# Where the buffers lie in SBUF: LayerNorm's little tiles go to the front, and 192 bytes are left free behind the x buffers

## The chip, the core and the metric

The kernel runs on one NeuronCore of a Trainium2 chip. The metric is device time in microseconds of one launch, from its begin to its end on the chip. The median of the runs is 721.3 us.

## What is computed

x is [2048, 512]. The rows are normalized, then go two ways: a Fourier mixing (a product with the 512-point DFT along the hidden axis and with the 2048-point DFT along the sequence, of which the real part is kept) and an MLP of width 1792 with a squared ReLU. The second gates the first.

```python
xn = _layernorm(x)                                # over the 512 features
a, b = xn @ dft_hid_re.T, xn @ dft_hid_im.T
s = dft_seq_re @ a - dft_seq_im @ b               # [2048, 512]
h = max(xn @ w1 + b1, 0) ** 2                     # [2048, 1792]
g = silu(h @ w2 + b2)
out = x + s * g
```

All inputs are float32.

## The kernel before

Nearly everything is a matmul of 128 x 128 weights (the stationary operand, read by a LDWEIGHTS of its own for each MATMUL) with 256 or 512 moving columns, both in float32 words ("fp32r") and both read from SBUF. To keep float32's precision, every operand is held as two parts, HI and LO, and every product is three passes: HI by HI, HI by LO, LO by HI. ScalarE writes HI (line 68) and VectorE LO (line 71). Most products also follow a scheme for 2 x 2 blocks that needs seven products instead of eight: the blocks and their sums are stored side by side in a buffer of seven slots. TensorE's order is written out by hand; the engines wait for each other by semaphores.

The stages, in order of time:

- **LayerNorm and the first two column chunks** (line 330, 384 matmuls of 512 columns). Stationary: the normalized x in eight buffers `XC[0..7]` (tags `xc0`..`xc7`, 14336 bytes in each partition). Moving: pieces of the sequence DFT matrix in the buffers `g1a`, `g1b`.
- **The other six column chunks** (function `mm`, line 277, 2016 matmuls of 256 columns; six chunks of eight steps of 42). Stationary: `XC`. Moving: products 1, 2, 3 take theirs from `g0a`/`g0b`, products 4, 5, 6, 7 from `g1a`/`g1b`. VectorE and ScalarE prepare the moving operands two steps ahead.
- **The hidden DFT** (`stage2`, line 263, 384 matmuls of 512 columns, laid between the steps of the others). Stationary: results of the stages above in the buffers `pq00`..`pq11`. Moving: the DFT matrix in `wd0`, `wd1`.
- **The first MLP layer** (`hidden`, line 517, 1176 matmuls of 256 columns): 4 token chunks of 7 units of 42. Stationary: w1, of which units 0 to 5 lie in `xc2`..`xc7` and unit 6 in `g0b` (3 slots, `w1a`) and `g1b` (4 slots, `w1b`). Moving: the normalized tokens `xT`, in `xc0`, `xc1` for chunks 0 and 2 and in `wd0`, `wd1` for chunks 1 and 3.
- **The second MLP layer** (`outer`, line 571, 1176 matmuls of 256 columns): 4 chunks of 7 units of 42. Stationary: h in `xc4`, `xc5`, `xc6`. Moving: w2, of which units 0 to 4 lie in `xc0`, `xc1`, `xc7`, `xc2`, `xc3` and units 5 and 6 in `wd0`, `wd1`.

One pool holds all of SBUF. It gives each tag its place the first time the tag is used, one behind the other, rounded up to 32 bytes. So the order in which tags first appear in the program settles every address. In the program before, `ln_stats` asks for its tile `bn` (three copies of 48 bytes, each on 64) and `ln_root` for `sm` (three copies of 16 bytes, each on 32) after `g0b` and before `g1a` have been placed: these 288 bytes lie between the two.

Of the kernel before, what the change touches and what calls it, by code (L numbers as in the profile page):

```python
# [7 lines left out]
F32 = mybir.dt.float32  # L8
# [4 lines left out]
P = 128  # L13
# [48 lines left out]
def fnet_gated_kernel(ctx, tc, x, xt, ct, wd, w1, w2, b1, b2, out):  # L62
# [10 lines left out]
    def split(*parts):  # L73
        split_hi(*parts)
        return split_lo(*parts)

    pool = ctx.enter_context(tc.tile_pool(name="pool", bufs=1))
# [17 lines left out]
    def buf(tag, shape, name, dtype=F32, bufs=1):  # L95
        return pool.tile(shape, dtype, tag=tag, bufs=bufs, name=name)

    def bcast(src, n):
        return bass.AP(tensor=src.tensor, offset=src.offset, ap=[[0, P], [1, n]])

    def halves(ap):
        return ap.rearrange("p (a b) -> p a b", a=2)


    XC = [buf(f"xc{j}", [P, 7, 2, 256], f"xc{j}", F32R) for j in range(NJ)]

    xr, xn32 = {}, {}

# [5 lines left out]

    def ln_stats(j, hs=slice(0, 2)):
        t = xr[j]
        sm = buf("bn", [P, 12], f"bn{j}_{hs.start}", bufs=3)
        for h in range(hs.start, hs.stop):
            bn = sm[:, 6 * h:6 * h + 6]
            nc.vector.bn_stats(bn, t[:, h])  # L120
            nc.vector.bn_aggr(stats[:, :, h, j], bn)

    root = {}

    def ln_root(j, hs=slice(0, 2)):
        n = hs.stop - hs.start
        t = root[j] = buf("sm", [P, 4], f"root{j}_{hs.start}", bufs=3)
        nc.scalar.activation(t[:, 0:n], stats[:, 1, hs, j], AF.Sqrt, bias=eps)

    def ln_rstd(j, hs=slice(0, 2)):  # L130
# [17 lines left out]
    def xc_parts(j, h):  # L148
        s = slice(2 * h, 2 * h + 2)
        return XC[j][:, s, HI, :], XC[j][:, s, LO, :], halves(xn32[j][:, h])  # L150

# [12 lines left out]
    def split_sums(j):  # L164
        s = xn32[j].rearrange("p h (b n) -> p (h b) n", b=2)
        split(XC[j][:, S2:S4 + 1, HI, :], XC[j][:, S2:S4 + 1, LO, :], s[:, 0:3])

    def split_s1(j):
        split(XC[j][:, S1, HI, :], XC[j][:, S1, LO, :], s1[j // ND][:, j % ND])

# [46 lines left out]
    def product(ms, n):  # L217
        m26, m753, m4, m1 = ms
        return {1: m1, 4: m4, 2: m26[:, 0], 6: m26[:, 1], 7: m753[:, 0], 5: m753[:, 1], 3: m753[:, 2]}[n]
# [30 lines left out]
    def pq(c, m, dh, src=None):  # L250
        t = PQ[c, m, dh] = buf(f"pq{m}{dh}", [P, 2, 512], f"pq{c}_{m}_{dh}", F32R)
        if src is not None:
            split(t[:, HI], t[:, LO], src)
        return t
# [18 lines left out]
    def mm(ps, w, mv, first, last):  # L273

        for d in range(2):
            for a_, b_ in PASSES:
                nc.tensor.matmul(ps[:, d * CW:(d + 1) * CW], w[:, a_, d * P:(d + 1) * P], mv(b_),  # L277
                                 start=first and d == 0 and (a_, b_) == (HI, HI),
                                 stop=last and (a_, b_) == (LO, HI), skip_group_check=True)
# [3 lines left out]
    def load_rows(c, t):  # L283

        flat = rows.rearrange("a b -> (a b)")
        for m in range(2):
            for h in range(2):
                n = m * S + c * TC + h * 256
                nc.sync.dma_start(t[:, 2 * m + 1 - h], bcast(flat[n:n + 256], 256))
        xT["rows"] = t  # L290
# [32 lines left out]
    def products(c, j, h, by_pass=False):  # L323

        g = part[c, j]
        for passes in [[q] for q in PASSES] if by_pass else [PASSES]:
            for k in range(ND):
                for a_, b_ in passes:
                    w = XC[j][:, 2 * h + k // 2, a_, k % 2 * P:(k % 2 + 1) * P]
                    nc.tensor.matmul(accs[c][k], w, g[:, b_, 2 * h:2 * h + 2],  # L330
# [6 lines left out]
    with tc.manual_schedule(engines=None):  # L337
# [10 lines left out]
        for n, (count, dtype) in enumerate(zip(WARM, (mybir.dt.bfloat16, F32R))):  # L348
            zeros = buf("g0" + "ab"[n], [P, 512], f"zeros{n}", dtype)
            nc.vector.memset(zeros if n == 0 else zeros.bitcast(F32), 0.0)  # L350
            for _ in range(count):
                nc.tensor.matmul(warm, zeros[:, 0:P], zeros, start=True, stop=True)
        plain_banks(0)
        ln_stats(0, one)
        ln_root(0, one)
        for h, hs in enumerate((one, two)):
            g = plain_parts(0, 0, hs)
            split_hi(*g)
            ln_rstd(0, hs)
            ln_xn(0, h)  # L360
            split_hi(*xc_parts(0, h))
            if h == 0:
                ln_stats(0, two)
                ln_root(0, two)
            split_lo(*g)
            if h == 1:
                ln_stats(1)
                g = plain_parts(0, 1)
                split_hi(*g)
                ln_root(1)  # L370
            split_lo(*xc_parts(0, h))
            products(0, 0, h, True)
        load_c(0, 3)
        load_x(4)
        for j in range(1, NJ):
            ln_rstd(j)
            for h in range(2):
                ln_xn(j, h)
                split_hi(*xc_parts(j, h))
            split_lo(*g)  # L380
            load_c(*order[j + 3])
            if j + 4 < NJ:
                load_x(j + 4)
            split_lo(*xc_parts(j, 0))
            if j + 1 < NJ:
                ln_stats(j + 1)
                ln_root(j + 1)
            xn_lo = split_lo(*xc_parts(j, 1))
            for h in range(2):
                products(0, j, h, j == 1)  # L390
            g = plain_parts(*order[j + 1])
            split_hi(*g)
            if j == 2:
                nc.sync.dma_start(b1s, b1)
                nc.sync.dma_start(b2s, bcast(b2, D))
        split_lo(*g)

    for n, (c, j) in enumerate(order):
# [20 lines left out]
        if j == NJ - 1:  # L419
            for dh in range(2):  # L420
                for m in range(2):
                    t = pq(c, m, dh)
# [216 lines left out]
    for c, j in steps:  # L639
# [3 lines left out]
        for p in ORDER:  # L643
            a, (grp, b) = PRODUCTS[p]
            mm(product(ms, p), XC[j][:, a], lambda b_: g[grp][:, b_, b], j == 0, j == NJ - 1)
        if c == PLAIN:
# [14 lines left out]
        if c == NC - 1:  # L661

            if j in (2, 3):
                q = j - 2
                t = buf(f"xc{2 + q}", [P, 3, 4, 256], f"stage{q}")
# [197 lines left out]
def _launch(arrays, out_shape):  # L863
    import numpy as np
    import concourse.bacc as bacc
    from concourse.bass_utils import run_bass_kernel_spmd

    nc = bacc.Bacc("TRN2", target_bir_lowering=False, num_devices=1, dynamic_dma_scratch_size=1024)
    feed, args = {}, []
    for name, v in arrays.items():  # L870
        v = np.ascontiguousarray(v)
        feed[f"in_{name}"] = v
        args.append(nc.dram_tensor(f"in_{name}", v.shape, mybir.dt.from_np(v.dtype), kind="ExternalInput").ap())
    args.append(nc.dram_tensor("out_0", out_shape, F32, kind="ExternalOutput").ap())
    with tile.TileContext(nc, schedule_with_timeline_sim=True) as tc:
        fnet_gated_kernel(tc, *args)
    r = run_bass_kernel_spmd(nc, [feed], core_ids=[0])
    return r.results[0]["out_0"]
# [25 lines left out]
```

## Time and profile before

| | |
|---|---|
| median of 3 runs | 721.3 us (721.28 to 721.83) |
| span of the profiled execution, first to last instruction | 719.5 us |
| TensorE busy with matmuls (PE) | 706.7 us, 5149 matmuls |
| TensorE busy with weight loads (PEld, beside PE) | 665.4 us, 5149 loads |
| VectorE (DVE) | 584.7 us |
| ScalarE (ACT) | 347.6 us |
| HBM read and written | 97.0 MB and 43.3 MB |

The profile is of one execution; its span is 1.8 us under the median of the runs, which also hold what lies before the first and after the last instruction. A matmul's duration in the records includes the time until its last column has left the array, and overlaps the next matmul's; what a matmul costs in a stream is the distance from its start to the next one's start. That is read here from rows of the timeline: the start of a row, the start of the next, and the count between.

### The profile page before, as it was taken

How to read it: one execution, taken by the hardware profiler on the slowest of the kernel's cores; microseconds unless marked ns; L12 is line 12 of the kernel's file. 1: busy time of each engine (PE TensorE's matmuls, PEld its weight loads, DVE VectorE, ACT ScalarE, POOL GpSimd, SP SyncE). 2: the span in 40 equal slices, each digit the busy share in tenths (PEclk: the TensorE clock that was granted, in tenths of full speed). 3: DMA queues.
4: the chain of work that ended last, by engine and by line, in shares of the span. 5: the costliest groups of instructions: out<-in, count | busy, mean ns of one | idle time of the engine just before them, and what ended most of it. 6: DMA issues, size and time to landing. Idle time of an engine off the chain costs nothing.

```text
span 719.5 us, 12692 instructions
## 1 busy us (share of the span) xinstructions
PE 706.7 (98%) x5149; PEld 665.4 (92%) x5149; DVE 584.7 (81%) x886; ACT 347.6 (48%) x475; POOL 5.2 (1%) x8
## 2 busy tenths in 40 slices
PE   8999999999999999999999999999999999999996
PEld 5778789999999999999998999999999999999996
DVE  7999554679598697797795955999988979989895
ACT  4438233434353544444542424777767764444441
POOL 0000000000000000000000000000000000101000
PEclk9999999999999999999999999999999999999999
DMA  9622540633553653744824669965625995767643
GB/s 325 217 88 89 169 137 16 220 107 128 206 205 132 218 189 122 273 152 139 298 92 147 224 243 337 352 248 205 255 112 188 343 405 196 187 205 199 219 146 111
DMA packets 55018, 141.09 MB, mean 196 GB/s; under 512 B 5040, under 2 KB 21680, under 8 KB 53680
## 3 DMA queue, kind: packets, MB, share of 16 engines
q1 hardware_dynamic: 49840, 124.56, 49.5%
q10 hardware_dynamic: 4032, 14.68, 5.2%
q0 software_dynamic: 1088, 1.05, 1.0%
q8 instruction: 40, 0.66, 0.3%
q14 instruction: 18, 0.15, 0.1%
HBM read 97.00 MB, written 43.27 MB: 195 GB/s over the span
## 4 chain that ended last, share of the span: by engine, by line
PE 83%; DVE 12%; issue 2%; ACT 1%; DMA 1%; DVEq 0%; ACTq 0%; SPq 0%
PE m_b L277 24%; PE yps L263 12%; PE m_b_o L571 10%; PE hps L517 9%; PE hps_b L517 5%; PE m_bb L277 5%; PE m_ba L277 5%; DVE g L71 3%; PE pq_b L330 3%; PE hps_ba L517 3%; DVE xc L71 2%; PE m_bc_o L571 1%; PE m_ba_o L571 1%; PE m_bb_o L571 1%; PE hps_bb L517 1%
## 5 line engine op out<-in xcount | busy, mean ns | idle before, releaser
L277 PE MATMUL m_b<-g,xc 128*128 128x256 f32 x1440 | 181.6, 281 | 0.0
L277 PEld LDWEIGHTS m_b<-g,xc 128*128 128x128 f32 x1440 | 175.7, 189 | 0.5
L71 DVE TENSOR_TENSOR g<-r,g 128x768 fp32r<-128x768 f32 (+2 forms) x65 | 65.5, 1007 | 45.4 <-ACT g L68 45.4
L68 ACT ACTIVATE g<-r 128x768 fp32r<-128x768 f32 (+2 forms) x65 | 57.4, 886 | 88.4 <-PE m_b L277 46.3
L263 PE MATMUL yps<-wd,pq 128*128 128x512 f32 x384 | 94.6, 395 | 0.0
L263 PEld LDWEIGHTS yps<-wd,pq 128*128 128x128 f32 x384 | 70.2, 188 | 15.2
L571 PE MATMUL m_b_o<-w,g 128*128 128x256 f32 x630 | 79.3, 282 | 0.5 <-ACT m_b_o L564 0.5
L571 PEld LDWEIGHTS m_b_o<-w,g 128*128 128x128 f32 x630 | 76.9, 191 | 0.7 <-ACT m_b_o L564 0.7
L71 DVE TENSOR_TENSOR g<-t,g 128x1024 fp32r<-128x1024 f32 x48 | 58.7, 1222 | 12.0 <-ACT g L68 12.0
L330 PE MATMUL pq_b<-g,xc 128*128 128x512 f32 x240 | 64.6, 399 | 2.9 <-DVE g L71 1.7
L517 PE MATMUL hps<-xT,w 128*128 128x256 f32 x504 | 61.9, 281 | 0.0
L517 PEld LDWEIGHTS hps<-xT,w 128*128 128x128 f32 x504 | 60.9, 190 | 0.1
L330 PEld LDWEIGHTS pq_b<-g,xc 128*128 128x128 f32 x240 | 44.1, 188 | 17.0 <-ACT xc L68 2.6
L68 ACT ACTIVATE g<-t 128x1024 fp32r<-128x1024 f32 x48 | 50.3, 1048 | 16.7 <-PE m_ba L277 6.8
L528 ACT ACTIVATE h<-h,b1s 128x512 f32<-128x512 f32 x56 | 37.4, 715 | 18.2 <-DVE h L229 18.2
L68 ACT ACTIVATE g<-hr 128x768 fp32r<-128x768 f32 (+1 forms) x28 | 35.5, 1266 | 21.0 <-DVE hr L196 6.7
L71 DVE TENSOR_TENSOR g<-hr,g 128x768 fp32r<-128x768 f32 (+1 forms) x28 | 41.6, 1485 | 2.2 <-ACT g L68 2.1
L277 PE MATMUL m_bb<-g,xc 128*128 128x256 f32 x288 | 43.3, 282 | 0.0
L277 PE MATMUL m_ba<-g,xc 128*128 128x256 f32 x288 | 42.9, 281 | 0.0
L277 PEld LDWEIGHTS m_bb<-g,xc 128*128 128x128 f32 x288 | 39.3, 189 | 1.8
L277 PEld LDWEIGHTS m_ba<-g,xc 128*128 128x128 f32 x288 | 38.1, 189 | 0.1
L188 DVE TENSOR_TENSOR t<-r 128x512 f32<-128x512 f32 x48 | 32.9, 685 | 5.0 <-DMA r<-in_ct 4.8
(167 smaller groups left out, 1007.7 us busy)
## 6 DMA issues: line engine op xcount, KB each, us to landing
r<-in_ct SPq DMA_DIRECT2D x63, 512.0 KB, 3.5
hd<-h ACTq DMA_DIRECT2D x28, 512.0 KB, 4.6
hr<-hd SPq DMA_DIRECT2D x28, 512.0 KB, 4.7
w1d<-w0g SPq DMA_DIRECT2D x21, 512.0 KB, 3.4
w<-w1d SPq DMA_DIRECT2D x6, 1792.0 KB, 9.3
w<-w2d SPq DMA_DIRECT2D x4, 1792.0 KB, 11.4
y<-ysb SPq DMA_DIRECT2D x16, 256.0 KB, 3.1
fin<-y SPq DMA_DIRECT2D x16, 256.0 KB, 5.1
```

Source lines behind the costliest of these rows:

```text
L68: nc.scalar.activation(hi, src, AF.Copy)
L71: return nc.vector.tensor_tensor(lo, src, hi.bitcast(F32), op=ALU.subtract)
L188: nc.vector.tensor_tensor(t[:, 0:2], r[:, 0:1].to_broadcast([P, 2, 256]), r[:, 1:3], op=ALU.add)
L263: nc.tensor.matmul(ps, PQ[c, m, k // 2][:, a_, w:w + P], WD[m, k][:, b_, :], start=n == 0, stop=n == 2 * ND * 3 - 1)
L277: nc.tensor.matmul(ps[:, d * CW:(d + 1) * CW], w[:, a_, d * P:(d + 1) * P], mv(b_), start=first and d == 0 and (a_, b_) == (HI, HI), stop= ...
L330: nc.tensor.matmul(accs[c][k], w, g[:, b_, 2 * h:2 * h + 2], start=j == 0 and h == 0 and (a_, b_) == (HI, HI), stop=j == NJ - 1 and h == 1 ...
L517: nc.tensor.matmul(product(ms, k), W1[p][a][:, a_, q * P:(q + 1) * P], xT[c, q][:, b_, b], start=share not in first, stop=q == 1 and (a_, ...
L528: nc.scalar.activation(x_[:, s], x_[:, s], AF.Relu, bias=b1s[:, f:f + 1])
L571: nc.tensor.matmul(m[:, k * 256:(k + 1) * 256], g[:, a_, a, k * P:(k + 1) * P], W2[p][:, b_, b], start=p == 0 and k == 0 and (a_, b_) == ( ...
```

## The change

The little tiles get their places right behind the statistics, ahead of `XC`, and a tile that nothing reads or writes stands behind `XC`.

```diff
+    small = {tag: [buf(tag, [P, n], f"{tag}_{i}", bufs=3) for i in range(3)] for tag, n in (("bn", 12), ("sm", 4))}
+
+    def few(tag, n, name):
+
+        return small[tag].pop(0) if small[tag] else buf(tag, [P, n], name, bufs=3)
...
     XC = [buf(f"xc{j}", [P, 7, 2, 256], f"xc{j}", F32R) for j in range(NJ)]
+
+    pool.tile([P, 48], F32, name="gap")
...
-        sm = buf("bn", [P, 12], f"bn{j}_{hs.start}", bufs=3)
+        sm = few("bn", 12, f"bn{j}_{hs.start}")
...
-        t = root[j] = buf("sm", [P, 4], f"root{j}_{hs.start}", bufs=3)
+        t = root[j] = few("sm", 4, f"root{j}_{hs.start}")
```

In the built programs, all engines have the same instructions in the same order with the same semaphores and the same addresses in HBM; only SBUF addresses differ. The first byte of a buffer in its partition:

| buffers | before | mod 256 | after | mod 256 |
|---|---|---|---|---|
| `xc0` (`xc1`.. follow at 14336) | 3552 | 224 | 3840 | 0 |
| `pq00`, `r`, `pq01`, `pq10`, `pq11` | 118240.. | 224 | 118720.. | 192 |
| `g0a`, `g0b` | 146912, 153056 | 224 | 147392, 153536 | 192 |
| `bn`, `sm` | 159200.. | | 3552.. | |
| `g1a`, `wd0`, `g1b`, `wd1`, `t`, `e`, `sx` | 159488.. | 0 | 159680.. | 192 |

Every slot that a matmul reads starts at a multiple of 512 bytes within its buffer. So for each stage there is one distance from the stationary to the moving operand, mod 256, whatever the slot:

| stage | stationary, moving | matmuls | columns | before | after |
|---|---|---|---|---|---|
| line 330 | `xc`, `g1` | 384 | 512 | 32 | 192 |
| line 277, products 1, 2, 3 | `xc`, `g0` | 864 | 256 | 0 | 192 |
| line 277, products 4, 5, 6, 7 | `xc`, `g1` | 1152 | 256 | 32 | 192 |
| line 263 | `pq`, `wd` | 384 | 512 | 32 | 0 |
| line 517, chunks 0, 2, units 0 to 5 | `xc`, `xc` | 504 | 256 | 0 | 0 |
| line 517, chunks 1, 3, units 0 to 5 | `xc`, `wd` | 504 | 256 | 32 | 192 |
| line 517, chunks 0, 2, unit 6: `w1a`; `w1b` | `g0b`; `g1b`, `xc` | 36; 48 | 256 | 0; 224 | 64; 64 |
| line 517, chunks 1, 3, unit 6: `w1a`; `w1b` | `g0b`; `g1b`, `wd` | 36; 48 | 256 | 32; 0 | 0; 0 |
| line 571, units 0 to 4 | `xc`, `xc` | 840 | 256 | 0 | 0 |
| line 571, units 5, 6 | `xc`, `wd` | 336 | 256 | 32 | 192 |

## The prediction

> **What bounds the kernel now.** I read the busy times first, then the stretches, then who waited for whom, and last the timeline of TensorE.
>
> ```profile
> PE 706.7 (98%) x5149; PEld 665.4 (92%) x5149; DVE 584.7 (81%) x886; ACT 347.6 (48%) x475; POOL 5.2 (1%) x8
> PEclk9999999999999999999999999999999999999999
> ```
>
> TensorE is busy for 98% of the span at its full granted clock. The stretches (columns: busy time of PE, PEld, DVE, ACT, POOL with counts, then granted clock, DMA share, GB/s) say where the missing 2% is:
>
> ```profile
> 0.00:72.10 72.10, 69.30 (x280) 51.92 (x280) 67.15 (x141) 37.02 (x64) 0.20 (x4) 1.00 0.50 179
> ...
> 112.40:418.70 306.30, 306.30 (x2306) 293.13 (x2305) 237.65 (x352) 132.80 (x179) 0.00 (x0) 1.00 0.49 173
> 418.70:569.60 150.90, 150.90 (x1225) 148.70 (x1225) 126.14 (x184) 96.99 (x135) 0.00 (x0) 1.00 0.67 249
> 569.60:719.50 149.90, 141.22 (x1178) 140.55 (x1176) 130.97 (x175) 68.61 (x80) 4.99 (x4) 0.99 0.65 213
> ```
>
> Up to 72 us VectorE sets the pace (67.15 of 72.10 us). From 112.4 to 569.6 us TensorE never stops, and VectorE has slack: 68.65 of 306.30 us in line 277's stretch, 24.76 of 150.90 us in line 517's. Of the waits that TensorE's matmuls have after the start, these are the longest:
>
> ```profile
> PE pq_b L330 <- DVE g L71: 1.7, 2, 1.3
> PE m L571 <- DVE g L71: 1.3, 1, 1.3
> ```
>
> So no load and no engine is waited for in the long middle. What can change there without any instruction changing is how long a matmul occupies TensorE. The timeline (start, us, row, count) shows that this isn't one number for 256 columns. First the second MLP layer, from the first row of a unit of 42 to the first row of the next:
>
> ```profile
> 580.53 0.88 PE L571 MATMUL m_bb_o<-w,g 128*128 128x256 f32 x6
> ...
> 585.57 0.88 PE L571 MATMUL m_bb_o<-w,g 128*128 128x256 f32 x6
> ...
> 595.65 0.88 PE L571 MATMUL m_bb_o<-w,g 128*128 128x256 f32 x6
> ...
> 600.61 0.87 PE L571 MATMUL m_bb_o<-w,g 128*128 128x256 f32 x6
> ...
> 605.55 0.88 PE L571 MATMUL m_bc_o<-w,g 128*128 128x256 f32 x6
> ```
>
> Unit 2 takes 585.57 - 580.53 = 5.04 us, 120.0 ns a matmul; units 5 and 6 together 605.55 - 595.65 = 9.90 us for 84, 117.9 ns. By the table of distances, unit 2 is at 0 and units 5 and 6 at 32. The first MLP layer says the same of chunk 0 (distance 0) and chunk 1 (distance 32):
>
> ```profile
> 450.00 0.88 PE L517 MATMUL hps_bb<-xT,w 128*128 128x256 f32 x6
> ...
> 455.04 5.20 PE L517 MATMUL hps<-xT,w 128*128 128x256 f32 x42
> ...
> 479.90 0.87 PE L517 MATMUL hps_bb<-xT,w 128*128 128x256 f32 x6
> ...
> 484.85 5.11 PE L517 MATMUL hps<-xT,w 128*128 128x256 f32 x42
> ```
>
> 5.04 us against 4.95 us, again 120.0 and 117.9 ns. That could still be a matter of where the moving operand alone lies. Unit 6 of chunk 1 decides it, since there the stationary operand lies in two places under one and the same moving operand:
>
> ```profile
> 494.75 1.58 PE L517 MATMUL hps<-xT,w1a 128*128 128x256 f32 x12
> 496.16 3.05 PE L517 MATMUL hps<-xT,w1b 128*128 128x256 f32 x24
> 499.04 0.86 PE L517 MATMUL hps<-xT,w1a 128*128 128x256 f32 x6
> ```
>
> `w1a`, at distance 32, takes 1.41 us for 12, 117.5 ns; `w1b`, whose both operands begin at a multiple of 256, takes 2.88 us for 24, 120.0 ns. So alignment as such buys nothing; distance 0 costs 2.1 ns more than distance 32. The loads fit that: 192 ns at distance 0 (`w1a` in chunks 0 and 2), 188 at 32 (`w1a` in chunks 1 and 3) and at 224 (`w1b` in chunks 0 and 2).
>
> ```profile
> L517 PEld LDWEIGHTS hps_ba<-xT,w1a x12: 192/192/193, 460.7 to 531.2; 128*128 128x128 f32 x12
> L517 PEld LDWEIGHTS hps<-xT,w1a x36: 187/188/189, 494.6 to 569.4; 128*128 128x128 f32 x36
> ...
> L517 PEld LDWEIGHTS hps_ba<-xT,w1b x12: 187/188/193, 461.4 to 531.9; 128*128 128x128 f32 x12
> ```
>
> My reading is that the read of the next weights and the stream of the moving columns get in each other's way when they start at the same place of some repeating pattern of SBUF. The Trainium skill has a sentence against this reading, in "TensorE: Matmul & The Clock Gate", section "Step-by-step: what each phase is for": TensorE has two separate read ports, and "Loading the next tile's weights doesn't steal SBUF read bandwidth from the running matmul." By that rule both distances should give one pitch, and the sum below would be 0; the trace disagrees, with 120.0 against 117.9 ns.
>
> **The change part by part.** It adds and removes no instruction, wait or transfer, so the sum is counts by differences in pitch. Line 277 now has a mixture of the two distances, and a step of 42 shows its mean; line 263 has 512 columns:
>
> ```profile
> 245.59 0.88 PE L277 MATMUL m_bb<-g,xc 128*128 128x256 f32 x6
> ...
> 250.57 0.88 PE L277 MATMUL m_bb<-g,xc 128*128 128x256 f32 x6
> ...
> 101.17 5.76 PE L263 MATMUL yps<-wd,pq 128*128 128x512 f32 x24
> 106.77 2.26 PE L330 MATMUL pq_b<-g,xc 128*128 128x512 f32 x9
> ```
>
> 4.98 us a step is 118.6 ns a matmul. For 512 columns it is 5.60 / 24 = 233.3 ns, which is 2 x 116.7: the loads are the same, but have twice the time, so I take 116.7 ns as what 256 columns cost when no weight load holds them up. At distance 32 the pitch of 117.9 still stands 1.2 ns above it.
>
> The unknown is p, the pitch of 256 columns at distance 192, which occurs nowhere in this trace. Its ends are 116.7 ns (no hold-up) and 120.0 ns (the same hold-up as at 0). Four terms follow:
>
> - Line 277, 2016 matmuls: 2016 x (118.6 - p).
> - Line 517, chunks 1 and 3, 504, and line 571, units 5 and 6, 336: 840 x (117.9 - p).
> - Unit 6 of the first MLP layer: 36 `w1a` matmuls of chunks 0 and 2 leave distance 0 and 36 of chunks 1 and 3 come to it, and 48 go from 224 to 64; I put this at nothing, and at 84 x 2.1 = 0.2 us at most.
> - Line 263, 384 matmuls, goes from 32 to 0. Costs lie between 0, if the longer stream covers the later load, and 384 x 2.1 = 0.8 us. I take half, 0.4 us. A gain isn't in it, since no row at distance 0 is faster than one at 32.
>
> Line 330's 384 matmuls go from 32 to 192 under VectorE's pace or at 233.3 ns, the floor as I read it: 0. The other 1344 matmuls of lines 517 and 571 stay at 0.
>
> VectorE and ScalarE read and write at other places too. Two forms of line 71 with equal size and different distances between their operands exist (`t`, `g1`: 0; `r`, `g1`: 32):
>
> ```profile
> L71 DVE TENSOR_TENSOR g<-t,g 128x1024 fp32r<-128x1024 f32 x48 | 58.7, 1222 | 12.0 <-ACT g L68 12.0
> L71 DVE TENSOR_TENSOR g<-r,g 128x1024 fp32r<-128x1024 f32 x15 | 18.3, 1219 | 0.3 <-ACT g L68 0.3
> ```
>
> 3 ns of 1219 on the 15 in VectorE's own stretch are 0.05 us: nothing. For transfers, 512 KB into `e`, a multiple of 256, land no sooner than 512 KB into `r`, 32 under one, so I expect nothing from the new places either:
>
> ```profile
> r<-in_ct SPq DMA_DIRECT2D x63, 512.0 KB, 3.5
> w0raw<-in_w SPq DMA_DIRECT2D x7, 512.0 KB, 4.5
> ```
>
> Which p? 192 is 64 away from a multiple of 256, twice as far as 32 is. If a hold-up that is whole at 0 is mostly gone 32 bytes off, the likeliest is that it isn't greater at 64; and 32 still leaves 1.2 ns. I take the middle between 116.7 and 117.9, p = 117.3: 2016 x 1.3 = 2.6 us, 840 x 0.6 = 0.5 us, less 0.4 us: 2.7 us gained. The profiled span of 719.5 us would go to 716.8, and the median, which lies 1.8 us higher, to 718.6 us. VectorE's slack covers it: line 277's stretch would lose 2.6 of 306.3 us.
>
> **The rivals.**
>
> 1. *192 is as good as 32 and no better* (p = 117.9). 2016 x 0.7 = 1.4 us gained, 0.4 lost: 720.3 us. For it: at 32 and at 224 (`w1b` in chunk 0) the load's length is alike, as if being off 0 were all that counts. Against: 117.9 is above the floor.
> 2. *The pattern repeats every 64 bytes* (p = 120.0). Then 192, three times 64, is distance 0 again, and only an odd multiple of 32 helps. Line 277 loses 2016 x 1.4 = 2.8 us, the 840 lose 840 x 2.1 = 1.8 us, line 263 0.4: 5.0 us, 726.3 us. Nothing in the trace speaks against it: all distances here are 0, 32 or 224. The change turns to a loss where p passes 118.25 ns: 2016 x 0.35 = 0.7 us gained, 840 x 0.35 = 0.3 us and line 263's 0.4 lost.
> 3. *The distance isn't the cause at all*, and nothing happens: 721.3 us. This is what follows if the two reads never meet, and the pitch differs by what the buffers hold. It has the `w1a`, `w1b` rows against it. The sentence of the Trainium skill quoted above would lead here.
>
> **How the numbers follow.** My forecast has 0.48, rival 1 0.24, rival 2 0.22, rival 3 0.05, and 0.01 is left for anything else. About 0.2% (1.4 us) is what a measurement of this kernel can tell from no change. The forecast is faster by 0.4%, and nearly all of its range is beyond 0.2%; rival 1, at 0.14%, is mostly within it. That makes 0.51 faster, 0.28 within, 0.21 slower. The forecast's own range is 716.0 to 719.9: with p at 116.7, 2016 x 1.9 + 840 x 1.2 = 4.8 us are gained, so 716.5, and a little room. Rival 2 holds more than 0.2, so the range must reach into it: a partial hold-up, p about 119.4, costs 2016 x 0.8 + 840 x 1.5 + 0.4 = 3.3 us, 724.6. I give 716.0 to 724.6.
>
> **What would show it.** In the trace after: a step of 42 at line 277 in 4.93 us (117.3 x 42) instead of 4.98; units of chunk 1 in line 517 at or under 4.95; units 0 to 4 of line 571 still at 5.04; 24 matmuls of line 263 in 5.60 to 5.65; all of unit 6 in chunk 1 at 120.0 ns. Steps of 5.04 at line 277 would mean rival 2, steps of 4.95 rival 1. The forecast is wrong if distance 192 falls on a repeat that I can't see from three distances, or if the hold-up isn't in the weights' read but in something that the new places change elsewhere.

## The result, and the profile after

The changed kernel takes 716.0 us (median of 4 runs, 715.8 to 716.5), against 721.3 us for the kernel before in the same rounds: a ratio of 0.9925 (95% interval 0.9911 to 0.9939), 5.3 us or 0.75% faster. The forecast was 718.6 us. The gain has the forecast's sign and about double its size, and most of it doesn't lie where the forecast put it.

The page after, busy times and the granted clock's line of the slices:

```profile
PE 700.7 (98%) x5149; PEld 661.2 (93%) x5149; DVE 584.7 (82%) x886; ACT 346.9 (49%) x475; POOL 5.2 (1%) x8
PEclk9999999999999999999999999999999999999998
```

TensorE lost 6.0 us of busy time with the same 5149 matmuls; VectorE has the same 584.7 us as before. The stretches (columns as in the prediction's; line numbers of the changed kernel are 8 higher):

```profile
0.00:112.10 112.10, 108.05 (x445) 83.11 (x446) 89.96 (x177) 49.12 (x82) 0.20 (x4) 1.00 0.49 167
112.10:415.30 303.20, 303.20 (x2305) 291.52 (x2304) 237.53 (x352) 132.01 (x179) 0.00 (x0) 1.00 0.52 175
415.30:565.40 150.10, 149.66 (x1227) 147.56 (x1226) 126.24 (x184) 97.25 (x136) 0.00 (x0) 1.00 0.69 250
565.40:714.00 148.60, 139.79 (x1178) 139.03 (x1176) 130.98 (x175) 68.57 (x80) 4.99 (x4) 0.99 0.67 215
```

Line 277's stretch, which holds line 263 too, went from 306.3 to 303.2 us, line 517's from 150.9 to 150.1, line 571's from 149.9 to 148.6. The first stretch lost 0.3 us (112.4 to 112.1). Together 5.5 us of span, 719.5 to 714.0.

Which matmuls did it is read from the timeline, from the start of a row to the start of the row that comes 42 (or 24) matmuls later. First a step of line 277 (now 285) and 24 matmuls of line 263 (now 271):

```profile
238.96 0.87 PE L285 MATMUL m_bb<-g,xc 128*128 128x256 f32 x6
...
243.91 0.87 PE L285 MATMUL m_bb<-g,xc 128*128 128x256 f32 x6
```
```profile
101.04 5.63 PE L271 MATMUL yps<-wd,pq 128*128 128x512 f32 x24
106.51 2.27 PE L338 MATMUL pq_b<-g,xc 128*128 128x512 f32 x9
```

A step takes 4.95 us, 117.8 ns a matmul, where it took 4.98. The 24 of line 263, now at distance 0, take 5.47 us, 227.9 ns each, where they took 5.60. Then the first MLP layer (line 517, now 525), a unit of chunk 1 and one of chunk 3. Both have distance 192, from the same buffers:

```profile
476.35 0.84 PE L525 MATMUL hps_bb<-xT,w 128*128 128x256 f32 x6
...
481.11 4.92 PE L525 MATMUL hps<-xT,w 128*128 128x256 f32 x42
...
545.50 0.87 PE L525 MATMUL hps_bb<-xT,w 128*128 128x256 f32 x6
...
550.45 5.11 PE L525 MATMUL hps<-xT,w 128*128 128x256 f32 x42
```

The first takes 4.76 us, 113.3 ns a matmul; the second 4.95 us, 117.9 ns. Line 571 (now 579) keeps its pitch at distance 0 and goes to the lower one at 192, from its unit 5 on:

```profile
576.28 0.88 PE L579 MATMUL m_bb_o<-w,g 128*128 128x256 f32 x6
...
581.32 0.88 PE L579 MATMUL m_bb_o<-w,g 128*128 128x256 f32 x6
...
591.40 0.86 PE L579 MATMUL m_bb_o<-w,g 128*128 128x256 f32 x6
...
596.18 0.84 PE L579 MATMUL m_bb_o<-w,g 128*128 128x256 f32 x6
...
600.94 0.87 PE L579 MATMUL m_bc_o<-w,g 128*128 128x256 f32 x6
```

Unit 2, at distance 0, still takes 5.04 us (120.0 ns). Units 5 and 6, at 192, take 4.78 and 4.76 us (113.6 ns on the mean). One new wait came: TensorE reaches unit 6 of chunk 0 before its weights are there (in brackets the idle time and what ended it).

```profile
458.42 0.97 PE L525 MATMUL hps_ba<-xT,w1b 128*128 128x256 f32 x6 [0.44 <-DMA w1b<-w1d]
459.23 2.28 PE L525 MATMUL hps_b<-xT,w1b 128*128 128x256 f32 x18
461.35 0.87 PE L525 MATMUL hps_b<-xT,w1a 128*128 128x256 f32 x6
...
527.94 2.20 PE L525 MATMUL hps_b<-xT,w1b 128*128 128x256 f32 x18
529.98 0.84 PE L525 MATMUL hps_b<-xT,w1a 128*128 128x256 f32 x6
```

The rows behind it show two pitches once more. Unit 6 has distance 64 in chunks 0 and 2. Behind the wait its 18 matmuls take 2.12 us in chunk 0 (117.8 ns); in chunk 2, without a wait, the same 18 take 2.04 us (113.3 ns).

### The profile page after: what moved, and what is told of

Its sections match the earlier page's. It is cut to its first block, busy times and chain, and to the rows that moved or that the text cites. A ratio compares the mean times of both kernels' runs of the same rounds, so it can differ in the third digit from the quotient of the medians.

```text
span 714.0 us, 12692 instructions
## 1 busy us (share of the span) xinstructions
PE 700.7 (98%) x5149; PEld 661.2 (93%) x5149; DVE 584.7 (82%) x886; ACT 346.9 (49%) x475; POOL 5.2 (1%) x8
## 4 chain that ended last, share of the span: by engine, by line
PE 79%; DVE 13%; DMA 4%; issue 2%; ACT 1%; SPq 0%; DVEq 0%; ACTq 0%
PE m_b L285 24%; PE yps L271 12%; PE m_b_o L579 10%; PE hps L525 7%; PE m_bb L285 5%; PE m_ba L285 5%; PE hps_b L525 4%; DMA w1b<-w1d 3%; DVE g L71 3%; PE pq_b L338 3%; PE hps_ba L525 2%; DVE xc L71 2%; PE m_bc_o L579 1%; DVE bn L128 1%; PE m_ba_o L579 1%
## 5 line engine op out<-in xcount | busy, mean ns | idle before, releaser
L271 PE MATMUL yps<-wd,pq 128*128 128x512 f32 x384 | 92.7, 391 | 0.0
```

Source lines behind the costliest of these rows:

```text
L271: nc.tensor.matmul(ps, PQ[c, m, k // 2][:, a_, w:w + P], WD[m, k][:, b_, :], start=n == 0, stop=n == 2 * ND * 3 - 1)
```

## The experiments

Pitches below are means from the trace, from one matmul's start to the next one's, over the matmuls of a form; where a row is shown, they can be worked out from it.

**m1: the stream alone, at every multiple of 32.** A kernel of matmuls only, with TensorE's pattern of line 277 (three passes, two halves, two weight slots) and the distance as a parameter; it leaves out everything of the reference. For each distance: 42 matmuls of 256 columns after a pause, 24 at distance 0 with 42 at the distance right behind, 12 of 512 columns at 0 with 42 behind, and 24 of 512 columns. In short form:

```diff
+for dist in range(0, 512, 32):
+    run(0, dist, 256, 42)
+    run(0, 0, 256, 24, close=False); run(1, dist, 256, 42)
+    run(0, 0, 512, 12, close=False); run(1, dist, 256, 42)
+    run(0, dist, 512, 24)
```

> Only matmuls in streams, nothing else of the computation; the output is a copy of x. The moving operand starts 0, 32, .. 480 bytes behind the stationary one (mod 512); per distance 42 matmuls of 256 columns after a pause, 42 directly after 24 at distance 0, 42 directly after 12 of 512 columns at distance 0, and 24 of 512 columns after a pause. Theory A (the read of the next weights can cost the stream a fixed number of cycles, and which cost it locks into depends on distance and on how the stream was entered): 0 gives 120.0 ns; 32 gives 117.8; 192 gives 113.3 or 117.8 depending on the entry; some distances give 113.3 on every entry; 512 columns give 227 or 233.3. Rival B (the pitch is a function of the distance alone): one value per distance, whatever the entry. Rival C (the other engines' work decides between 113.3 and 117.8): here, where they rest, every distance but 0 gives 113.3.

Measured, ns a matmul in the steady part:

| distance | after a pause | behind 24 at 0 | behind 512 columns | 512 columns |
|---|---|---|---|---|
| 0 | 120.0 | 120.0 | 120.0 | 227.3 |
| 32 | 116.8 | 117.7 | 116.7 | 233.4 |
| 64 | 117.8 | 117.8 | 117.8 | 228.7 |
| 96 | 120.1 | 119.9 | 119.9 | 233.2 |
| 128 | 119.9 | 118.7 | 119.9 | 231.9 |
| 160 | 117.3 | 117.3 | 118.6 | 234.5 |
| 192 | 117.8 | 113.3 | 117.8 | 233.4 |
| 224 | 118.2 | 118.3 | 118.3 | 233.4 |

256 to 480 give the same numbers as 0 to 224. The rows of distances 0, 32, 192 and 256 in the timeline (42; 24 and 42 in one row of 66; 24 of 512):

```profile
22.14 5.30 PE L49 MATMUL k<-V,W 128*128 128x256 f32 x42 [0.33 <-ACT scrap L51]
27.75 8.17 PE L49 MATMUL k<-V,W 128*128 128x256 f32 x66 [0.32 <-ACT scrap L51]
...
44.68 5.74 PE L49 MATMUL k<-V,W 128*128 128x512 f32 x24 [0.38 <-ACT scrap L67]
50.68 5.16 PE L49 MATMUL k<-V,W 128*128 128x256 f32 x42 [0.26 <-ACT scrap L51]
...
72.88 5.86 PE L49 MATMUL k<-V,W 128*128 128x512 f32 x24 [0.38 <-ACT scrap L67]
...
193.00 5.21 PE L49 MATMUL k<-V,W 128*128 128x256 f32 x42 [0.26 <-ACT scrap L51]
198.54 7.90 PE L49 MATMUL k<-V,W 128*128 128x256 f32 x66 [0.32 <-ACT scrap L51]
...
215.42 5.86 PE L49 MATMUL k<-V,W 128*128 128x512 f32 x24 [0.69 <-ACT scrap L67]
...
250.01 5.30 PE L49 MATMUL k<-V,W 128*128 128x256 f32 x42 [0.26 <-ACT scrap L51]
...
272.56 5.74 PE L49 MATMUL k<-V,W 128*128 128x512 f32 x24 [0.38 <-ACT scrap L67]
```

A row's length holds some 0.26 us beyond count times pitch, the end of its last matmul's record: 5.30 us is 42 x 120.0 ns and 0.26. The two rows of 66 have the same first 24 matmuls, so the 0.27 us between 8.17 and 7.90 belong to the other 42: 6.4 ns each, the step from 120.0 to 113.6. VectorE and GpSimd have no work beside these streams, and ScalarE only a short read behind each; transfers end at about 35 us, and distance 256 repeats the numbers of 0 without them. So what the other engines do is not the cause. Distance alone isn't it either: 192 gives 117.8 or 113.3 by what ran before. And 512 columns are the other way round: fastest at distance 0.

**e1: the little tiles in front, without the gap.** All buffers then start at a multiple of 256, and every distance is 0.

```diff
-    pool.tile([P, 48], F32, name="gap")
```

> The little tiles in front, but no gap: every buffer that a matmul reads starts at a multiple of 256, distance 0 everywhere. Theory A (distance decides): all matmuls of 256 columns at 120.0 ns. Against the changed kernel line 277's 2016 lose 2.2 ns each (4.4 us), chunks 1 and 3 of line 517 and units 5 and 6 of line 571 about 4.5 us, line 330's matmuls past 73 us gain about 0.8 us at 227.5 ns: about 724 us. Rival (alignment to 256 bytes is what helped, not distance): 716 us or less.

724.55 us (724.46 to 724.72), ratio 1.004 (1.0025 to 1.0055): slower than before. Line 277 runs at 119.9 ns, line 263 at 228.1 ns:

```profile
100.44 5.60 PE L270 MATMUL yps<-wd,pq 128*128 128x512 f32 x24
105.89 2.20 PE L337 MATMUL pq_b<-g,xc 128*128 128x512 f32 x9
```

5.45 us for 24 is 227.1 ns. So the layout with all buffers aligned to 256 bytes costs about 3 us, line 263's gain and a wait of 1.1 us for `w1b` included.

**e2: the gap alone**, the little tiles where they were. `xc` to `g0` is then at 192, `xc` to `g1` and `wd` at 224, and line 263 stays at 32.

```diff
     XC = [buf(f"xc{j}", [P, 7, 2, 256], f"xc{j}", F32R) for j in range(NJ)]
+    pool.tile([P, 48], F32, name="gap")
```

> The gap alone; the little tiles stay between g0b and g1a. Distances: g0 to xc 192, g1 and wd to xc 224, wd to pq 32. Theory A: line 277 at 117.8 ns as in the changed kernel; line 263 back at 233.3 ns (2.2 us lost against the changed kernel), chunks 1 and 3 of line 517 and units 5 and 6 of line 571 at 117.8 ns (2.4 us lost): about 720.6 us. Rival (the gap alone makes the gain, the place of the little tiles counts for nothing): 716 us.

720.34 us (720.09 to 720.89), ratio 0.9985 (0.9975 to 0.9994). Line 277 runs at 117.9 ns on the mean, line 517's chunks 1 and 3 and line 571's units 5 and 6 at 118.3, and line 263 keeps its pitch:

```profile
101.00 5.76 PE L265 MATMUL yps<-wd,pq 128*128 128x512 f32 x24
106.61 1.79 PE L332 MATMUL pq_b<-g,xc 128*128 128x512 f32 x7
```

5.61 us for 24 is 233.8 ns. With e1 this shows that line 263's gain comes from the move from 32 to 0, and that neither half of the diff brings the change's gain: the tiles alone lose 2.9 us, the gap alone gains 1.3.

**e3: a gap of 64 bytes.** Whatever is at 192 in the changed kernel is at 64, and line 263 at 0 as there.

```diff
-    pool.tile([P, 48], F32, name="gap")
+    pool.tile([P, 16], F32, name="gap")
```

> As the changed kernel, but 64 bytes in the gap instead of 192: distance 64 where it was 192. Theory A with a pattern that is the same in both directions or repeats every 128 bytes: as the changed kernel, 716 us within 1.5. Rival (192 is special): line 277 at 117.8 to 120.0 ns and the other streams slower than 114 ns, 718 to 724 us.

717.53 us (716.30 to 718.11), ratio 0.9940 (0.9925 to 0.9955), 1.5 us behind the changed kernel. Line 277 runs at 117.75 ns and line 263 at 228.1, as there. Line 517's chunk 1 (117.8) and line 571's units 5 and 6 (117.9) don't have the 113.3 ns that they have there: 252 and 336 matmuls by 4.4 and 4.1 ns are 2.5 us. The run is 1.0 us better than that. In the traces line 330's 384 matmuls take 0.8 us less together (229.1 ns against 233.3 where nothing holds them), the wait for `w1b` isn't there, and line 263 loses 0.3 us. The pitches are the rival's, the time lies just under its range. Distance 64 has a fast pitch too (113.3 ns in unit 6 of chunk 2 of the changed kernel); these streams don't reach it, and in m2 a stream that enters 64 as they do stays at 117.8.

**m2: what lets a stream at 192 run at 113.3 ns.** Again matmuls alone, in parts one behind the other, given as (distance, columns, count), in short form and not all of them.

```diff
+[(0, 512, 12), (0, 256, n), (192, 256, 42)]        # n = 1, 2, 3, 6, 12, 24
+[(d, 256, 24), (192, 256, 42)]                     # d = 32, 64, 96, 128, 160, 224
+[(0, 256, 6), (192, 256, 36)] * 4
+[(0, 256, 24), (d, 256, 42)]                       # d not a multiple of 32
```

> Only matmuls in streams, as in the sweep; the output is a copy of x. Streams at distance 192 are entered from 1, 2, 3, 6, 12 or 24 matmuls of 256 columns at distance 0 that follow 12 of 512 columns; from other distances; and streams change between 0 and 192 every 3, 6 or 18 matmuls. Theory A (two locked states at 192, and the distance-0 stream ahead leads into the fast one): from some small count on, 192 runs at 113.3 ns; below it at 117.8. Theory A': it takes a long distance-0 stream; 1 to 12 matmuls still give 117.8. Distances that aren't multiples of 32: no expectation, they show how wide the fast state's window is.

One matmul of 256 columns at 0 ahead leaves 192 at 117.8 ns; two or more give 113.3. So do 24 at 96, 128 or 160, and not those at 32, 64 or 224. A stream at 64 behind 24 at 0 stays at 117.8. Where 24 of 512 columns stand between two streams at 192, the second runs at 113.4 ns if they are at 192 too, and at 117.8 if they are at 0 or 64. The rows for 64 and 96 (24 matmuls and the 42 at 192 in one row):

```profile
110.12 8.04 PE L68 MATMUL k<-V,W 128*128 128x256 f32 x66 [0.32 <-ACT scrap L72]
118.47 7.91 PE L68 MATMUL k<-V,W 128*128 128x256 f32 x66 [0.32 <-ACT scrap L72]
```

The second has the slower first 24 (119.9 against 117.8 ns) and is the shorter one. Six at 0 suffice to put the next 36 at 113.3 ns, again and again. Of the distances between, 112 gave 113.3 ns after a pause and behind 0; 16 after a pause only; 184, 196 and 200 gave 120.0 behind 0, so the good places are narrow. Three streams at 192 right after a pause also ran at 113.3 ns here, against 117.8 in m1.

**e4: one x buffer at distance 0, ahead of the fast steps.** From m2 I concluded that it is enough to have some matmuls at 0 ahead of a stream at 192, so `xc3` alone goes behind the gap: step 3 of each chunk at 0, steps 4 to 7 at 192.

```diff
+    BEHIND = (3,)
-    XC = [buf(f"xc{j}", ...) for j in range(NJ)]
+    XC = {j: buf(f"xc{j}", ...) for j in range(NJ) if j not in BEHIND}
     pool.tile([P, 48], F32, name="gap")
+    XC |= {j: buf(f"xc{j}", ...) for j in BEHIND}
```

> As the changed kernel, but of the eight x buffers xc3 alone is placed behind the gap, so that line 277's step j = 3 is at distance 0 and steps 4 to 7 come after it at 192. Theory A (the stream ahead decides between 117.8 and 113.3 ns at 192): steps 4 to 7 of all six chunks at 113.3 (168 x 6 x 4.5 ns = 4.5 us gained), step 3 at 120.0 (0.6 us lost), line 571's unit 4 at 113.3 (1.1 us gained), unit 5 of line 517 about even: 711 us. Rival (what else the engines do in line 277's stage holds it at 117.8): steps 4 to 7 stay at 117.8, and with the other terms 715.5 us.

715.46 us (715.06 to 715.62), ratio 0.9918 (0.9901 to 0.9934): the rival's 715.5, not 711. The steps of line 277 behind step 3 don't change:

```profile
142.76 0.87 PE L287 MATMUL m_bb<-g,xc 128*128 128x256 f32 x6
...
147.71 0.87 PE L287 MATMUL m_bb<-g,xc 128*128 128x256 f32 x6
```

4.95 us, 117.9 ns. Unit 4 of line 571, whose moving operand is `xc3` and which came to 192, did run at 113.8 ns, and line 517's units 5 and 6 of chunks 0 and 2, at 64, at 113.3; its chunk 1 went back to 117.8. My conclusion from m2 fell: a stretch at 0 ahead is not enough.

**e5: three x buffers behind the gap**, the same test with more places where 0 and 192 meet.

```diff
-    BEHIND = (3,)
+    BEHIND = (0, 1, 3)
```

> As the changed kernel, but xc0, xc1 and xc3 are placed behind the gap. Theory A: line 277's steps 0, 1, 3 at 120.0, step 2 at 117.8, steps 4 to 7 at 113.3 ns (2.9 us gained in all); line 517's units 0 to 4 at 113.3 in chunks 1 to 3 and 117.8 in chunk 0, units 5 and 6 at 120.0 (2.0 us gained); line 571's units 0, 1, 4, 5, 6 at 113.3, 2 and 3 at 120.0 (3.4 us gained): 708 us. Rival (pitch by distance alone, 117.8 at 192): 715 to 716 us.

718.06 us (716.00 to 719.22), ratio 0.9951 (0.9934 to 0.9969): slower than both numbers, for a reason apart from the pitches. Line 277's 756 matmuls at 0 take 119.7 ns and its 1260 at 192 take 117.8, none of them 113.3; line 517's chunk 1 is back at 117.8 (252 x 4.4 ns = 1.1 us). Line 571's units 0 and 1, now at 192, run at 116 to 118 ns in chunks 0 and 1 and at 113.3 to 114.4 in chunks 2 and 3. The end is longer: behind its wait for VectorE, here of 1.79 us, TensorE's granted clock is at half for a while. First that stretch, then the 64 matmuls behind the wait, here and in the changed kernel:

```profile
694.50:698.00 3.50, 3.50 (x19) 3.50 (x18) 2.70 (x4) 0.00 (x0) 0.00 (x0) 0.51 1.06 357
```
```profile
693.96 9.34 PE L581 MATMUL m<-w,g 128*128 128x256 f32 x64 [1.79 <-DVE g L71]
```
```profile
693.10 7.66 PE L579 MATMUL m<-w,g 128*128 128x256 f32 x64 [1.34 <-DVE g L71]
```

That is 1.7 us. The run of 716.00 us has a mean granted clock of 0.998, the other three (717.7 to 719.2 us) have 0.994. So without the lower clock this layout takes about what the rival says, 715 to 716 us, and theory A's 708 fails all the same. Why the mean clock is lower in three runs of four is not known.

**m3: whose place jumps.** In m2 the stationary operand stayed and the moving one jumped; in e4 it was the other way round. m3 gives each a place of its own: (stationary, moving, columns, count).

```diff
+[(0, 0, 256, 24), (0, 192, 256, 42)]        # the moving operand jumps
+[(192, 192, 256, 24), (0, 192, 256, 42)]    # the stationary one jumps
+[(64, 64, 256, 24), (0, 192, 256, 42)]      # both
+[(192, 192, 512, 24), (0, 192, 256, 42)]    # line 263 ahead of line 277
+[(192, 192, 512, 24)] + [(0, 0, 256, 6), (0, 192, 256, 36)] * 3
...
```

> Only matmuls in streams; the output is a copy of x. In the kernel with xc3 behind the gap, line 277 went from distance 0 to 192 and stayed at 117.8 ns, where the earlier streams by themselves went to 113.3: there the stationary operand changed its place, in the streams the moving one did. Theory D (the jump of the moving operand brings the fast state): 0 to 192 gives 113.3 when the moving operand's place changes by 192, 117.8 when the stationary one's does. Rival E (something else in the kernel holds line 277): both give 113.3. Line 263's stream ahead of 192 gives 117.8 by both; six matmuls at 0 by the moving operand's place ahead of 36 at 192, three times over, give 113.3 in the 36 by theory D.

In turn: 113.3, 117.8, 113.3, 117.8, and 113.3 in each of the three parts of 36. The second and third test have one row each:

```profile
31.53 8.07 PE L65 MATMUL k<-V,W 128*128 128x256 f32 x66 [0.26 <-ACT scrap L69]
39.92 7.90 PE L65 MATMUL k<-V,W 128*128 128x256 f32 x66 [0.32 <-ACT scrap L69]
```

Both have 24 matmuls at distance 0 and 42 at 192 with the same 42 addresses; 0.17 us between them is 4 ns on each of the 42. The second test is e4's case and gives e4's pitch; the fourth is line 277 behind line 263 and gives line 277's. The places by themselves don't count: the first 24 of the first three tests, with both operands at 0, at 192 and at 64, all run at 119.6 to 120.0 ns.

**e6: line 277 entered by the moving operand.** If a jump of the moving operand from distance 0 sets the fast pitch, line 277 needs a product whose moving operand lies at 0. Product 1's gets a buffer of its own, ahead of the gap; the others stay at 192. ScalarE and VectorE each split the group in two pieces now; each has 50 operations more.

```diff
+    zero = [buf("gz" + "ab"[n], [P, 512], f"zeros{n}", dtype) ...]
     pool.tile([P, 48], F32, name="gap")
...
-        g0 = buf(f"g0{k}", [P, 2, 3, CW], f"g0_{key}", F32R)
+        z = buf(f"gz{k}", [P, 2, CW], f"gz_{key}", F32R)
+        g0 = buf(f"g0{k}", [P, 2, 2, CW], f"g0_{key}", F32R)
...
-        split(g0[:, HI], g0[:, LO], r[:, I11:I21 + 1])
+        split(z[:, HI], z[:, LO], r[:, I11])
+        split(g0[:, HI], g0[:, LO], r[:, I22:I21 + 1])
...
```

> As the changed kernel, but the moving operand of line 277's product 1 has a buffer of its own ahead of the gap, so that product 1 (6 of 42 matmuls) is at distance 0 and the other six products at 192: the moving operand jumps in each step. ScalarE and VectorE split that buffer in 48 instructions more each, 0.2 us apiece, beside TensorE. Theory D: product 1 at 118 to 120 ns, the others at 113.3 to 114, 114.3 on average: 2016 x 3.4 ns = 6.9 us gained on the changed kernel, 709 us; less where VectorE or a load then is late. Rival E (line 277 is held at 117.8 by something else): product 1 at 120.0, the others at 117.8: 716.6 us.

711.12 us (710.84 to 711.42), ratio 0.9854 (0.9838 to 0.9871): 4.9 us better than the change. A step of line 277:

```profile
147.72 0.88 PE L288 MATMUL m_bb<-gz,xc 128*128 128x256 f32 x6
...
152.55 0.87 PE L288 MATMUL m_bb<-gz,xc 128*128 128x256 f32 x6
```

4.83 us, 115.0 ns. Over the stage the 288 of product 1 take 118.1 and the other 1728 114.15 ns, a mean of 114.7 against 117.74: 2016 x 3.04 = 6.1 us. Line 517's chunk 1 went back to 117.8 ns and gave 1.1 us of it back.

**e7: the same, and another slot of the last weights in the buffer ahead.** Unit 6 of the first MLP layer has one slot in `gzb`. In e6 it is the slot of the unit's first product, here that of its last one, so that the six matmuls ahead of chunks 1 and 3 are at distance 0 and the moving operand jumps behind them. Against e6:

```diff
-            nc.sync.dma_start(z.bitcast(F32), W1D[p][:, :, 0])
-            nc.sync.dma_start(a.bitcast(F32), W1D[p][:, :, 1:3])
+            nc.sync.dma_start(z.bitcast(F32), W1D[p][:, :, 2])
+            nc.sync.dma_start(a.bitcast(F32), W1D[p][:, :, 0:2])
...
```

> As e6_gz, but of w1's unit 6 the slot that the unit's last product reads (A22) lies in the buffer ahead of the gap, instead of the first one's (A11). In chunks 0 and 2 the last six matmuls ahead of the next chunk then are at distance 0 with the stationary operand where the next chunk has it, and the moving operand jumps by 192. Theory D: chunks 1 and 3 of line 517 go from 117.8 to 113.3 ns, 504 x 4.5 ns = 2.3 us gained: 708.8 us. Rival (chunk 1's pace is settled by the wait for the load of w1's unit 6 or by other work): 117.8 stays, 711.1 us.

709.51 us (708.94 to 711.40), ratio 0.9832 (0.9818 to 0.9845). Both chunks run at 113.5 ns. A unit of chunk 1, in e6 first:

```profile
460.47 0.87 PE L530 MATMUL hps_bb<-xT,w 128*128 128x256 f32 x6
...
465.42 5.11 PE L530 MATMUL hps<-xT,w 128*128 128x256 f32 x42
```
```profile
462.15 0.84 PE L530 MATMUL hps_bb<-xT,w 128*128 128x256 f32 x6
...
466.91 4.92 PE L530 MATMUL hps<-xT,w 128*128 128x256 f32 x42
```

4.95 us became 4.76. This is the best version: 11.8 us under the kernel before, 6.5 us under the change. Its profile is of the execution of 711.40 us, and has 1.7 us of waits more than e6's: 1.0 for `w1b`, and 0.7 more for ScalarE in line 571.

## Why the prediction was right and wrong

The terms, in us, negative where time is saved; the measured ones are counts by differences of mean pitch in the two traces:

| term | forecast | measured | pitch before and after, ns |
|---|---|---|---|
| line 277, 2016 | -2.6 | -1.7 | 118.58, 117.74 |
| line 517, chunks 1 and 3, and line 571, units 5 and 6, 840 | -0.5 | -2.45 | 117.85; then 113.4 (chunk 1), 117.8 (chunk 3), 113.8 (line 571) |
| line 263, 384 | +0.4 | -1.9 | 233.4, 228.4 |
| unit 6 of line 517 | 0 | +0.5 | with the wait for `w1b` |
| line 330 | 0 | 0 | VectorE's pace for most of it |
| sum | -2.7 | -5.6 | span: -5.5 |

Two terms gained more than forecast, by 2.3 and 1.95 us, and two less, by 0.9 and 0.5; the total hides that in part.

- **Failed: "I take 116.7 ns as what 256 columns cost when no weight load holds them up."** It was half of 233.3 ns, read from 512-column matmuls at distance 32, on the ground that the loads have twice the time there. The 512-column stream was itself held up: at distance 0 it takes 227.3 ns, half of which is 113.7, and 256 columns do go down to 113.3. The floor was at least 3.4 ns too high, and two terms hang on it. The 840 could not gain more than 1.2 ns each by my bounds, and 588 of them gained 4 to 4.4. For 252 of these, chunk 1's, the gain (1.1 us) was luck: chunk 3 has the same places and got nothing, and ahead of chunk 1 stands the wait for `w1b`, which the forecast didn't have.
- **Failed by the same step: line 263's sign.** "A gain isn't in it, since no row at distance 0 is faster than one at 32" was true of 256 columns alone; there was no row of 512 columns at distance 0. The nearest row was of another shape, and at the other shape the order is reversed. This is the largest miss, 2.3 us, and e1 and e2 show it by itself: 5.45 us for 24 at distance 0, 5.61 at 32.
- **Failed in form: p as one number.** I took the middle of 116.7 and 117.9. Distance 192 has two steady pitches, 117.8 and 113.3 at the same addresses. Line 277 got the upper one, 117.74, which is the number of rival 1, and its step of 4.95 us is what the prediction named as rival 1's mark. The term came out 0.9 us short.
- **Right in the main: the distance is the cause**, with what ran ahead, and neither alignment nor another engine. m1 shows it with TensorE alone, and e1, which has everything aligned, is slower than before. That the weights' read is one side of it fits a pitch that changes with the stationary operand's place alone (`w1a` and `w1b` before; in m3, with the moving operand at 0, 119.6 ns with the stationary one at 0 and 117.8 at 64). No run has a stream without loads, so the hold-up itself is argued. The sentence of the Trainium skill that a load of weights takes no bandwidth from the running matmul ("TensorE: Matmul & The Clock Gate", "Step-by-step: what each phase is for") doesn't fit these streams: 113.3 to 120.0 ns for the same work.
- **Right:** streams that stay at distance 0 stay at 120.0 ns (line 571's units 0 to 4), all of unit 6 in chunk 1 went there, and VectorE's slack covered the gain: 584.7 us of work in both, and no new wait for it in the middle.
- **Rival 2 was wrong in its period, right in its fear.** The pattern repeats every 256 bytes, not every 64: neither 192 nor 64 is like 0 (120.0 ns). But 96 and 128 are as bad as 0 behind a pause (120.1 and 119.9), so a place off 0 could have gained nothing.
- **Unit 6** was put at nothing, and no transfer was to change. Its matmuls at 64 got faster (4.76 us for the 42 in chunk 2), but the wait in chunk 0 costs more than that saved. Line 463's (now 471's) transfer of `w1b` was issued 3.3 us earlier (435.8 us against 439.1) and took 1.9 us longer, while TensorE came some 3.6 us earlier. Had it taken as long as before, it would have landed at 456.5 us, ahead of TensorE. From issue to landing, before and after:

```profile
DMA to landing us min/median/max: 20.7/20.7/20.7
```
```profile
DMA to landing us min/median/max: 22.6/22.6/22.6
```

Over the versions it took 20.4 (e6) to 23.0 us (e1). Whether the places have a part in that is not shown.

What stays open: which entry leads to which of the two pitches. Where two or more matmuls of 256 columns at distance 0 stood ahead and the moving operand jumped to 192, 113.3 to 114.2 ns followed in every case here (m1, m2, m3, line 571, e6, e7); behind 512 columns at 0 it was 117.8 (m1). Where only the stationary operand jumped to 192, it was 117.8 (m3, e4). Where both jump, or behind a pause, both results occur. Chunks 1 and 3 of line 517 are entered from stationary 192 and moving 0 in the changed kernel. Chunk 1 follows a unit 6 that ran at 117.8 ns since the wait, and ran at 113.4; chunk 3 follows one at 113.3, and ran at 117.8, as both did in e4 behind units at 113.3. But in e6 chunk 1 follows a unit 6 at 117.8 and ran at 117.8 too, so this isn't the whole rule.

The entries on record also fit another reading than theory D's, and no run separates the two. In the tests at 192 the moving operand jumped by 192 bytes and the stationary one by 64 (from 192 to 0, which is 256 mod 256, or from 0 to 64). At distance 64 it is the other way round: from distance 0, a stationary operand that jumps by 192 leads to 113.3 ns (unit 6 of chunk 2 in the changed kernel, line 517's unit 5 in e4), and a moving one that jumps by 64 to 117.8 (m2, line 571 in e3). So it may be the size of the jump that counts, and not which operand makes it.

What in SBUF or in TensorE makes these two states was not measured; the runs show pitches only.

## What to carry to other kernels

Where TensorE never waits and each matmul has its own weights, measure the pitch from start to start and set it against the places of both operands mod 256: here 6% lay in it, free of any instruction. Try the offset with a few streams of matmuls alone before choosing a layout, with 256 and 512 columns apart and with what runs ahead of them, since the best place for one shape was the worst for the other. And don't take a floor from the fastest row that a trace happens to have: a row is a floor only if something else shows that nothing holds it up.

## What the runs showed of the hardware

- A matmul of 256 float32 columns with a load of 128 x 128 weights ahead of each takes 113.3 to 120.1 ns, one of 512 columns 227.3 to 234.5 ns, by the difference of the two operands' places mod 256 and what ran ahead, with VectorE and GpSimd at rest (m1).
- For 256 columns distance 0 is among the worst (120.0), for 512 it is the best of the multiples of 32 (227.3).
- At distances 192 and 64 two pitches are each stable for dozens of matmuls at the same addresses (117.8 and 113.3 ns), and the matmuls ahead decide; two of 256 columns at distance 0 sufficed for 113.3 at 192 (m2).
- 4 and 8 bytes off 192 (196; 184, 200), behind 24 matmuls at 0, the pitch is 120.0 ns, where 192 gives 113.3.
- After a wait of 1.79 us TensorE's granted clock was 0.51 for 3.5 us (e5); after one of 1.34 us at the same place the 64 matmuls took 7.66 us instead of 9.34.
